# A short convolution and a spectral mix on one core: instruction order by hand, spectrum layouts and the band of the convolution changed

## The chip, the cores and the metric

The kernel runs on one core of one Trainium2 chip. The metric is the device time of one execution in microseconds; the time of a kernel is the median of its runs. A core has the engines TensorE (PE, whose weight loads are listed as PEld), VectorE (DVE), ScalarE (ACT), GpSimd (POOL) and SyncE (SP), each with its own queue that it issues in order. DMA transfers here are issued from POOL's queue (input x and the weights, with a cast from float32 to bfloat16) and from SP's queue (the filter and the output).

## The reference

Eight sequences of 3264 positions with 192 channels pass through two layers. The first is a causal convolution over 7 positions; each of 8 heads of 24 channels has one filter, normalised by a softmax. The second keeps the 64 lowest Fourier modes along the sequence, mixes the channels of each mode by a complex 192 x 192 matrix of its own, transforms back, and ends with a residual branch.

```python
# layer 1: x (8, 3264, 192), weight (8 heads, 7)
w = exp(weight - max(weight, -1)); w = w / (sum(w, -1) + 1e-09)
out = np.einsum('hk,bskhg->bshg', w, x_unf)     # x_unf: the 7 last positions
x = out.reshape(B, S, D)

# layer 2: w_r, w_i (64 modes, 192, 192), w_ch (192, 192)
X = np.fft.rfft(x, axis=1);  Xr, Xi = real and imaginary part of X[:, :64]
Yr = np.einsum('bmd,mde->bme', Xr, w_r) - np.einsum('bmd,mde->bme', Xi, w_i)
Yi = np.einsum('bmd,mde->bme', Xr, w_i) + np.einsum('bmd,mde->bme', Xi, w_r)
y = np.fft.irfft(Y, n=S, axis=1)                # Y is zero above mode 63
u = x + y
return u + np.maximum(u @ w_ch, 0.0)
```

## The kernel before

A batch is cut into 27 windows of 122 positions, each loaded with 6 positions of overlap ahead of it into 128 partitions of `x_all`. The unit of work is 10, 8 or 9 windows of a batch, 24 units in all, and each unit's load is one DMA issued on POOL (`load_unit`, L61).

*Setup.* `cband` (L123, L126) holds for each head a 128 x 128 band matrix with the filter's 7 values on its diagonals. It is built on DVE from seven masks (`maskk`, made on POOL at L105): one scaling and six multiply-adds for each head. `fst` is the DFT basis, 27 windows of 64 cosine and 64 sine columns: DVE computes the angle in five passes (L141 to L150, tiles `kprod` and `turns`), ACT takes Abs and two Sin (L152 to L154).

*Conv and DFT.* `conv_unit` takes a unit in two halves of four heads: four matmuls into a PSUM tile of a pool with two buffers (`cp`, L220), and an ACT copy back over `x_all` as bfloat16 (L226). For the first unit of a batch it first zeroes six rows of overlap on DVE (L215), once that unit has landed. `dft(b)` accumulates 27 matmuls of a batch (L272), casts the result to `xs` (L275), and `xtrans` turns it by six small matmuls into `xt`, the mixing's operand (L282 to L286). In program order dft(b) comes two batches behind the conv.

*Mixing and transposes.* 16 groups take four modes each: twelve matmuls (L321) of `xt` with the weights of two tiles `wt`, of which six buffers exist and 32 are loaded (L201); an ACT cast to `ymix`; two transposes, whose results go to `yeT` for two groups at once, one half by DVE (L343), one by ACT (L345), written with a stride. Between these stand `t_unit`, which transposes the conv's result into `cT` for the output (a tail copy `tl` on DVE, L233 to L236, 12 to 15 transposes on PE, L264, and two DVE copies, L266), and `g_part`, which transposes `fst` into the inverse basis `gst`.

*Output.* `zwi_pair` makes the mixed spectra of two batches, with and without `w_ch`, from `yeT` (L363 to L371). An item is two windows of two batches: `group_z` multiplies the inverse basis and `cT` into a PSUM tile (L379 to L386), ACT takes the maximum with zero in place (L388), `group_y` adds the rest (L393), DVE adds x into `t` (L404), and SP stores `t` after two items (L410). PSUM tiles here, those of `zwi_pair` (`zwps`) too, come from one pool of four buffers. group_y runs two items behind group_z in program order.

*The order.* Nothing above fixes the order on an engine. A planner orders the instructions of each engine by the program's order as a priority and by a model of when each is ready, so that instructions can pass each other; semaphores follow from the data.

## Time and profile before

| What | Value |
|---|---|
| median of 3 runs | 252.18 us |
| lowest, highest | 250.66, 253.94 us |
| the profiled execution: its own time | 252.29 us |
| its span, first to last instruction | 250.6 us |
| busy in the span: PE, DVE, ACT, POOL | 171.6, 131.7, 106.3, 69.7 us |
| mean granted PE clock | 0.890 of full speed |
| moved by DMA | 40.50 MB; 40.31 MB read from and 20.05 MB written to HBM |
| the chain that ended last, by engine | PE 50%, DMA 23%, DVE 7%, ACT 6%, POOL 5% |

All times in profile rows are microseconds from the span's start unless marked ns. A row of groups gives line, engine, operation, output and inputs, shapes and count, then busy time and mean of one in ns, then idle time of the engine just before them and what ended it. A row of a timeline gives start, length, engine, line and operation; the bracket at its end is the idle time before it and what ended that. L12 is line 12 of the kernel.

### The profile page before, as it was taken

The numbers are of one execution on the slowest core, as the hardware profiler recorded it, in microseconds if no ns is written. First come the engines' busy times: TensorE is split into PE (matmuls) and PEld (weight loads), VectorE is DVE, ScalarE is ACT, GpSimd is POOL, SyncE is SP. The second block draws the span as 40 slices with busy tenths as digits, with TensorE's granted clock in tenths as the row PEclk, the third lists the DMA queues.
The fourth block names the chain that finished last, engine by engine and source line by source line (L and its number), as shares of the span: only waits on it lengthen the run. The fifth ranks groups of instructions, "written<-read, shape, count | busy, mean of one in ns | idle before, by whom it ended". The sixth has DMA issues, their size and how long they took to land.

```text
span 250.6 us, 4371 instructions
## 1 busy us (share of the span) xinstructions
PE 171.6 (68%) x1699; PEld 130.4 (52%) x1699; DVE 131.7 (53%) x246; ACT 106.3 (42%) x140; POOL 69.7 (28%) x118
## 2 busy tenths in 40 slices
PE   0126604705999997797886359998798769978910
PEld 0014403604998995565653127886576447756700
DVE  4999022013334568589985121676656165756530
ACT  2025907502999935211221223655355345544510
POOL 8964445342900006756658100000000000000000
PEclk9999955665999999799999556999999999999995
DMA  4999999999980005999999900599898758799791
GB/s 37 171 188 191 192 192 192 192 192 188 132 137 1 3 3 67 179 191 158 160 166 157 157 0 0 150 258 263 218 253 230 208 158 237 214 257 255 203 260 56
DMA packets 65340, 40.50 MB, mean 162 GB/s; under 512 B 31016, under 2 KB 65320, under 8 KB 65320
## 3 DMA queue, kind: packets, MB, share of 16 engines
q0 software_dynamic: 37600, 20.14, 61.0%
q1 hardware_dynamic: 27720, 20.09, 29.0%
q8 instruction: 13, 0.21, 0.4%
q14 instruction: 7, 0.06, 0.1%
HBM read 40.31 MB, written 20.05 MB: 241 GB/s over the span
## 4 chain that ended last, share of the span: by engine, by line
PE 50%; DMA 23%; DVE 7%; ACT 6%; POOL 5%; issue 4%; SPq 1%; DVEq 0%; ACTq 0%; POOLq 0%
DMA x_all<-in_x_dram 19%; PE zp L379 7%; PE zp L386 7%; PE zp L384 7%; PE xp L272 7%; PE zp L393 6%; PE cp L220 5%; PE tp L264 5%; ACT zp L388 4%; DMA wt<-in_moe_w_i_dram 4%; DVE cT L266 4%; PE yp L321 2%; POOL x_all L61 2%; POOL wt L201 2%; SPq L410 1%
## 5 line engine op out<-in xcount | busy, mean ns | idle before, releaser
L404 DVE TENSOR_TENSOR t<-zp,x_all 122x768 f32<-122x768 f32 (+1 forms) x54 | 50.7, 955 | 33.2 <-PE zp L393 19.4
L388 ACT ACTIVATE zp<-zp 128x768 f32<-128x768 f32 x54 | 42.9, 795 | 40.9 <-PE zp L386 40.9
L226 ACT CAST x_all<-cp 122x960 bf16<-122x960 f32 (+2 forms) x48 | 39.4, 884 | 31.2 <-PE cp L220 30.9
L384 PE MATMUL zp<-win,cT 128*128 128x192 bf16 x216 | 45.8, 251 | 0.0
L220 PE MATMUL cp<-x_all,cband 128*128 128x240 bf16 (+2 forms) x192 | 30.2, 291 | 20.6 <-DVE cband L126 16.5
L379 PE MATMUL zp<-zwi,gst 128*128 128x384 bf16 x108 | 36.2, 335 | 3.7 <-ACT zwi L371 3.7
L220 PEld LDWEIGHTS <-cband 128*128 128x128 bf16 x192 | 19.8, 109 | 26.4 <-DVE cband L126 17.8
L393 PE MATMUL zp<-zwi,gst 128*128 128x384 bf16 x108 | 25.4, 324 | 8.8 <-ACT zp L388 8.8
L201 POOL DMA_DIRECT2D wt<-in_moe_w_r_dram x32 | 19.5, 610 | 42.4 <-PE yp L321 35.5
L266 DVE COPY cT<-tp 128x854 bf16<-128x854 bf16 (+2 forms) x48 | 28.3, 612 | 4.2 <-PE tp L264 3.7
L264 PE MATMUL tp<-ident,tl 122*128 122x122 bf16 x112 | 22.0, 227 | 10.1 <-DVE tl L233 9.8
L264 PE MATMUL tp<-ident,x_all 122*128 122x122 bf16 x216 | 26.3, 228 | 3.5 <-DVE cT L266 2.9
L61 POOL DMA_DIRECT2D x_all<-in_x_dram x24 | 23.6, 994 | 17.2 <-DMA x_all<-in_x_dram 17.1
L272 PE MATMUL xp<-x_all,fst 122*128 122x192 bf16 (+1 forms) x216 | 25.1, 263 | 0.8 <-ACT fst L154 0.8
L386 PEld LDWEIGHTS <-cT 128*128 128x128 bf16 x216 | 21.6, 100 | 7.6 <-issue 0.8
L384 PEld LDWEIGHTS <-cT 128*128 128x128 bf16 x216 | 21.6, 100 | 7.0 <-issue 4.7
L386 PE MATMUL zp<-win,cT 128*128 128x192 bf16 x112 | 23.6, 250 | 0.0
L386 PE MATMUL zp<-wB,cT 128*128 128x192 bf16 x104 | 22.2, 253 | 0.0
L264 PEld LDWEIGHTS <-x_all 122*128 122x128 bf16 x216 | 18.3, 103 | 7.4 <-issue 5.8
L272 PEld LDWEIGHTS <-fst 122*128 122x128 bf16 (+1 forms) x216 | 20.1, 105 | 2.1 <-ACT fst L154 1.2
L201 POOL DMA_DIRECT2D wt<-in_moe_w_i_dram x32 | 19.9, 621 | 2.2 <-DMA x_all<-in_x_dram 1.4
L326 ACT CAST ymix<-yp 128x192 bf16<-128x192 f32 x16 | 5.2, 327 | 34.5 <-PE yp L321 34.4
(82 smaller groups left out, 168.7 us busy)
## 6 DMA issues: line engine op xcount, KB each, us to landing
out_dram<-t SPq DMA_DIRECT2D x48, 336.0 KB
wt<-in_moe_w_r_dram POOLq DMA_DIRECT2D x32, 144.0 KB, 5.0
wt<-in_moe_w_i_dram POOLq DMA_DIRECT2D x32, 144.0 KB, 5.1
x_all<-in_x_dram POOLq DMA_DIRECT2D x8, 432.0 KB, 16.7
x_all<-in_x_dram POOLq DMA_DIRECT2D x9, 384.0 KB, 17.9
x_all<-in_x_dram POOLq DMA_DIRECT2D x7, 480.0 KB, 18.4
out_dram<-t SPq DMA_DIRECT2D x48, 30.0 KB
out_dram<-t SPq DMA_DIRECT2D x8, 168.0 KB
```

Of the source, the lines that this page charges most:

```text
L201: nc.gpsimd.dma_start(out=wt[64 * half:64 * half + 64, :, :, :], in_=src[MG * g:MG * g + MG, :, :].rearrange("m (p j) e -> p m j e", j=3))
L220: nc.tensor.matmul(cp[:, j, 0:GRP * n].rearrange("p (w e) -> p w e", w=n), cband[:, h, :], x_all[:, b, w0:w0 + n, GRP * h:GRP * h + GRP], ...
L226: nc.scalar.copy(out=dst, in_=srcv)
L264: nc.tensor.transpose(tp[:, WIN * k:WIN * k + WIN], slot_lhsT(b, u, tl, a + k), ident[0:WIN, 0:WIN])
L266: nc.vector.tensor_copy(out=cT[:, b, WIN * a:WIN * (a + cnt)], in_=tp[:, 0:WIN * cnt])
L272: nc.tensor.matmul(xp[:, 0:D], fst[0:k, c, :], x_all[0:k, b, c, :], start=(c == 0), stop=(c == NWIN - 1))
L379: nc.tensor.matmul(zp[:, k, 0:2 * D], gst[:, WIN * w:WIN * w + P], zwi[:, 2 * q:2 * q + 2, 0, :], start=True, stop=False, skip_group_check ...
L384: nc.tensor.matmul(o, cT[:, b, WIN * sa:WIN * sa + P], win0[:, 0:D], start=False, stop=False, skip_group_check=True)
L386: nc.tensor.matmul(o, cT[:, b, WIN * sb:WIN * sb + P], wBs[par], start=False, stop=(i == 1), skip_group_check=True)
L388: nc.scalar.activation(out=zp[:, :, 0:2 * D], in_=zp[:, :, 0:2 * D], func=ACT.Relu)
L393: nc.tensor.matmul(zp[:, k, 0:2 * D], gst[:, WIN * w:WIN * w + P], zwi[:, 2 * q:2 * q + 2, 1, :], start=False, stop=True, skip_group_check ...
L404: nc.vector.tensor_tensor(out=tv, in0=yv, in1=xv, op=ALU.add)
```

## The change

- Every engine issues in the order in which the program emits its instructions (`manual_schedule`); the program's order is rewritten for that.
- Setup: the two index rows are made first on POOL; the masks stand behind the loads of the first two units. `cband` is zeroed, and each diagonal of four heads is written at once by a copy under a mask; the filter's values stand in a PSUM tile (`wps`). The angle's passes follow on DVE without anything between; its three ACT functions (`make_f`) stand behind the evictions of the fourth conv unit.
- The DFT goes by units: `dft_unit` follows the conv with a lag of five units at first and one at the end; `xtrans` comes one unit after the batch's cast.
- Layouts: `fst` has cosine and sine of a mode side by side, and two selecting matrices `sel` take the place of `ident` and `perm` in `xtrans`. `xt` is laid out with the mode innermost, so that the copy into it is written in runs of 64 and the matmuls read its 32 columns 64 elements apart. `yeT` is laid out by mode and then part and batch; each group's two transposes go there by one DVE copy, and `zwi_pair` reads its columns 8 elements apart.
- Mixing: the weights of the third next group are asked for behind a group's matmuls. All transposes follow the spectrum, two units a group in the first eight groups and one in the next seven; `g_part` comes from the ninth group on.
- Output: the next `zwi_pair` follows the item of window 12 of a pair of batches in place of window 4.

```diff
+    ctx.enter_context(tc.manual_schedule())
...
-        for h in range(H):
-            nc.vector.tensor_scalar(out=cband[:, h, :], in0=maskk[:, 0, :], scalar1=wsb[:, h, 0:1],
-                                    scalar2=None, op0=ALU.mult)
-            for k in range(1, KK):
-                nc.vector.scalar_tensor_tensor(out=cband[:, h, :], in0=maskk[:, k, :],
-                                               scalar=wsb[:, h, k:k + 1], in1=cband[:, h, :],
-                                               op0=ALU.mult, op1=ALU.add)
+    nc.vector.memset(cband[:], 0.0)
...
+    wps = pxx.tile([P, 512], F32, tag="xp", name="wps")
+    wsb = wps[:, 0:H * KK].rearrange("p (h k) -> p h k", h=H)
...
+    for half in range(2):
+        hs = slice(4 * half, 4 * half + 4)
+        for k in range(KK):
+            nc.vector.copy_predicated(
+                out=cband[:, hs, :],
+                mask=maskk[:, k, :].bitcast(mybir.dt.uint16).unsqueeze(1).to_broadcast([P, 4, P]),
+                data=wsb[:, hs, k:k + 1].to_broadcast([P, 4, P]))
...
+    def make_f():
+        nc.scalar.activation(out=turns[:], in_=kprod[:], func=ACT.Abs)
+        nc.scalar.activation(out=fst[:, :, 1:2 * MODES:2], in_=kprod[:], func=ACT.Sin, scale=-TWOPI / S)
+        nc.scalar.activation(out=fst[:, :, 0:2 * MODES:2], in_=turns[:], func=ACT.Sin, scale=-TWOPI / S,
+                             bias=halfpi[:, 0:1])
...
-    xt = ep.tile([P, 3, MODES + 1, 2 * B], BF16, tag="xt")
+    xt = ep.tile([P, 4, 2 * B, MODES], BF16, tag="xt")
...
-    yeT = constp.tile([P, 2, B, 2 * MODES], BF16, tag="yeT")
+    yeT = constp.tile([P, 2, MODES, 2 * B], BF16, tag="yeT")
...
+    def dft_unit(b, u):
+        w0, n = UNITS[u]
+        if u == 0:
+            xps[b] = pxx.tile([P, 512], F32, tag="xp", name="xp")
+        xp = xps[b]
+        for c in range(w0, w0 + n):
             k = WIN if c < NWIN - 1 else LASTVALID
             nc.tensor.matmul(xp[:, 0:D], fst[0:k, c, :], x_all[0:k, b, c, :],
                              start=(c == 0), stop=(c == NWIN - 1))
+        if u == 2:
+            xs = workp.tile([P, D], BF16, tag="xs")
+            nc.vector.tensor_copy(out=xs[:], in_=xp[:, 0:D])
+            xps[b] = xs
...
+            for v in range(2):
+                nc.tensor.matmul(tp[64 * v:64 * v + 64, j, :], xsv[:, j, :], sel[:, v, :],
+                                 start=True, stop=True, tile_position=(0, 64 * v))
+        nc.vector.tensor_copy(out=xt[:, 0:3, b:2 * B:B, :],
+                              in_=tp[:, :, :].rearrange("p j (c m) -> p j c m", c=2))
...
+    for i, (b, u) in enumerate(units):
+        conv_unit(b, u)
+        if i == 3:
+            make_f()
+            setup_stack.close()
+        if xq:
+            xtrans(xq.pop(0))
+        dq.append((b, u))
+        lag = max(1, 5 - i // 4)
+        while len(dq) > lag:
+            db, du = dq.pop(0)
+            dft_unit(db, du)
+            if du == 2:
+                xq.append(db)
+    for db, du in dq:
+        dft_unit(db, du)
+        if du == 2:
+            xq.append(db)
+    for b in xq:
+        xtrans(b)
...
-                                 xt[:, j, m:m + 2, :].rearrange("p m k -> p (m k)"),
-                                 wt[:, m % MG, j, :], start=(j == 0), stop=(j == 2),
-                                 tile_position=(0, 32 * pos))
+                                 xt[:, j:j + 2, :, m].rearrange("p j k -> p (j k)"), wt[:, m % MG, j, :],
+                                 start=(j == 0), stop=(j == 2), tile_position=(0, 32 * pos))
+        for i in range(4 // MG):
+            n = 6 + (4 // MG) * g + i
+            if n < NGRP:
+                load_weights(n)
         ymix = workp.tile([P, D], BF16, tag="ymix")
         nc.scalar.copy(out=ymix[:], in_=yp[:, 0:D])
-        if tq:
-            t_unit(*tq.pop(0))
-        if gq:
+        for _ in range(2 if g < 8 else 1):
+            if tq and g < NG4 - 1:
+                t_unit(*tq.pop(0))
+        if gq and g >= 8:
             g_part(gq.pop(0))
...
+        nc.vector.tensor_copy(out=yeT[:, :, 4 * g:4 * g + 4, :],
+                              in_=et[:, :, :].rearrange("p t (q k) -> p t q k", q=4)[:, :, :, 0:16])
+        if g == NG4 - 2:
+            while tq:
+                t_unit(*tq.pop(0))
...
-        if item[2][0][1] == 4 and done_q + 1 < B // 2:
+        if item[2][0][1] == 12 and done_q + 1 < B // 2:
```

217 lines of the change are left out of this document (90 added, 127 removed).

## The prediction

> **What bounds the kernel now.** I read the busy times by stage first, because the share of the whole span hides that the stages have different limits. Columns: stage, its length, busy time (instructions) of PE, PEld, DVE, ACT and POOL, granted PE clock, DMA share, GB/s.
>
> ```profile
> 0.00:59.60 59.60, 19.18 (x114) 13.51 (x114) 26.77 (x91) 21.01 (x22) 32.95 (x55) 0.79 1.46 173
> 59.60:95.20 35.60, 34.44 (x387) 31.06 (x385) 17.31 (x17) 27.81 (x34) 6.42 (x11) 0.96 0.45 64
> 95.20:146.70 51.50, 37.52 (x537) 25.67 (x538) 34.86 (x81) 12.22 (x26) 30.37 (x52) 0.88 0.99 150
> 146.70:157.80 11.10, 9.72 (x56) 6.71 (x57) 2.97 (x4) 3.71 (x6) 0.00 (x0) 0.66 0.00 0
> 157.80:250.60 92.80, 70.75 (x611) 53.43 (x608) 49.82 (x54) 41.55 (x53) 0.00 (x0) 0.96 0.79 217
> ```
>
> Stage 1 loads x while PE is busy 19 of 60 us; stage 2 has PE busy 34 of 36 us and moves almost nothing; stage 3 streams the mixing weights; stage 4 starts the output, stage 5 stores it. So the work of stage 2 could lie beside the load of stage 1. The views of tile kprod (duration min/median/max in ns, first and last start) and of the waits (total, times, longest), and PE's timeline, say why it doesn't:
>
> ```profile
> L141 DVE TENSOR_TENSOR kprod<-sidx,midx x1: 1954/1954/1954, 20.5 to 20.5; 128x1728 f32<-128x1728 f32 x1
> L145 DVE TENSOR_SCALAR turns<-kprod x1: 1331/1331/1331, 22.5 to 22.5; 128x1728 f32<-128x1728 f32 x1
> L149 DVE TENSOR_TENSOR kprod<-kprod,turns x1: 1882/1882/1882, 31.1 to 31.1; 128x1728 f32<-128x1728 f32 x1
> L150 DVE TENSOR_SCALAR kprod<-kprod x1: 983/983/983, 38.0 to 38.0; 128x1728 f32<-128x1728 f32 x1
> L152 ACT ACTIVATE fst<-kprod x1: 1643/1643/1643, 39.1 to 39.1; 128x1728 bf16<-128x1728 f32 x1
> L153 ACT ACTIVATE turns<-kprod x1: 1626/1626/1626, 40.6 to 40.6; 128x1728 f32<-128x1728 f32 x1
> ```
>
> ```profile
> DVE x_all L215 <- DMA x_all<-in_x_dram: 28.7, 6, 6.4
> ```
>
> ```profile
> 44.76 4.21 PE L272 MATMUL xp<-x_all,fst 122*128 122x192 bf16 x27 [0.84 <-ACT fst L154]
> 48.81 0.68 PE L220 MATMUL cp<-x_all,cband 128*128 128x192 bf16 x6
> 59.15 0.32 PE L282 MATMUL tp<-ident,xs 128*64 128x128 bf16 x1 [9.66 <-DVE xs L275]
> ```
>
> DVE issues in order, and between the passes that build the DFT basis stand the small memsets of L215, each of which waits for a batch that has not landed: 28.7 us in six waits. The basis is therefore complete only at 44.7, and then PE waits another 9.7 us for a cast behind one more such memset. The load itself never pauses; its last piece lands at 63.1, where POOL's queue is released:
>
> ```profile
> 63.09 0.58 POOL L201 DMA_DIRECT2D wt<-in_moe_w_r_dram  x1 [1.49 <-DMA x_all<-in_x_dram]
> ```
>
> **Stage by stage, the change.** *The conv band.* Removed: 8 + 48 DVE passes over 128 numbers, which run from 5.6 to 20.6. Added: a memset and 14 predicated copies of 512 numbers, data in PSUM.
>
> ```profile
> L126 DVE SCALAR_TENSOR_TENSOR cband<-maskk,wsb,cband x48: 340/347/423, 6.1 to 20.3; 128x128 bf16<-128x128 bf16 x48
> L123 DVE TENSOR_SCALAR cband<-maskk,wsb x8: 251/419/679, 5.6 to 17.2; 128x128 bf16<-128x128 bf16 x8
> ```
>
> ```profile
> L404 DVE TENSOR_TENSOR t<-zp,x_all 122x768 f32<-122x768 f32 (+1 forms) x54 | 50.7, 955 | 33.2 <-PE zp L393 19.4 <-DMA out_dram<-t 12.1 <-ACT zp L388 1.4
> ```
>
> ```profile
> L321 PEld LDWEIGHTS <-xt x192: 92/96/151, 95.2 to 144.4; 128*32 128x32 bf16 x192
> L321 PE MATMUL yp<-wt,xt x192: 246/256/368, 95.2 to 144.5; 128*32 128x192 bf16 x192
> L286 DVE CAST xt<-tp x8: 1774/1796/1802, 59.7 to 93.4; 128x384 bf16<-128x384 f32 x8
> ```
>
> No row shows a predicated copy. The nearest is L404, two operands with one in PSUM: 955/768 = 1.24 ns a number, so 0.64 us each. The far end is L286, whose target is scattered: 1796/384 = 4.7 ns, 2.4 us each. A copy could hardly be quicker than L126's 347 ns. I take 0.64, since source and target run on in the free dimension; 14 cost 9.0 us. From about 6.0 (the masks now stand behind four loads on POOL, and each copy needs only its own mask) the band is done at 15.0, its first half at 10.5.
>
> *The basis.* L141 moves ahead, into the time in which DVE waits for the filter. The other passes follow the band with no memset between: 1.33 + 0.98 (the middle one counted like L150) + 1.88 + 0.98 = 5.2, to 20.2. On ACT the basis stands behind the evictions of four conv units, and the fourth unit's memset behind this chain on DVE; x is no hindrance, as 37 of 216 windows have landed by a sixth of 63.1. A microsecond for memset and first matmuls and 1.6 for its two evictions bring 22.8; table load, Abs and two Sin cost 1.28 + 1.63 + 1.64 + 1.64 = 6.2, so the basis is there at 29.0, not 44.7.
>
> ```profile
> 30.17 1.28 ACT L152 ACT_TABLE_LOAD   x1
> ```
>
> ```profile
> 65.00 4.80 ACT L226 CAST x_all<-cp 122x768 bf16<-122x768 f32 x6 [0.58 <-PE cp L220]
> 70.14 4.80 ACT L226 CAST x_all<-cp 122x768 bf16<-122x768 f32 x6 [0.34 <-PE cp L220]
> ```
>
> What is late next is ACT. In the old stage 2, conv and DFT together went at one batch (six evictions) in 70.14 - 65.00 = 5.14 us, 1.71 a unit, with PE full. Twenty units are left at 29.0: 34.3 us, to 63.3, which is just when the last x lands (63.1, plus the little that two iotas ahead of the first load take). Queued behind the basis on ACT are these evictions, and behind them conv and DFT on PE, so every microsecond that the band costs more moves this end by as much; that is the sensitive term. PE begins the DFT after a pause, and a batch of it took 4.21 us there (PE rows above), where conv and DFT of a batch together later took 5.14; I add 1.5 for that start. The last unit then needs its second eviction, nine DFT matmuls, cast, six transposing matmuls and the xt copy, now with runs of 64: about 3.5 us in all. The spectrum is complete at 63.3 + 1.5 + 3.5 = 68.3 instead of 95.2: a gain of 27.
>
> *Mixing and transposes.* All 24 units of transposes now come after the spectrum; before, some had been done early. A group mixes four modes, and the first eight groups carry two units each.
>
> ```profile
> 125.41 1.18 DVE L266 COPY cT<-tp 128x976 bf16<-128x976 bf16 x2
> 126.50 0.28 DVE L235 COPY tl<-x_all 122x512 bf16<-122x512 bf16 x1
> ```
>
> ```profile
> 129.88 0.60 PE tp L264 x8
> ```
>
> In the old order the tail copy of the next unit stood ahead of this unit's two copies (the tails of two buffers alternate). Written out by hand it stands behind them, and PE must wait for it with six of eight transposes: 0.28 + 0.49 + 1.09 = 1.85 us a unit, where DVE alone would need 1.4. With the one yeT copy (its 16-long runs cost me 0.3, not the 0.75 of before) a group takes 4.0, so the eighth ends at 68.3 + 32 = 100.3. Up to there the weights keep ahead; from there a group has one unit (2.4 us, basis transposes included) and the weights are late:
>
> ```profile
> 141.32 0.67 PE L321 MATMUL yp<-wt,xt 128*32 128x192 bf16 x10 [1.10 <-DMA wt<-in_moe_w_i_dram]
> ...
> 144.22 0.67 PE L321 MATMUL yp<-wt,xt 128*32 128x192 bf16 x10 [1.11 <-DMA wt<-in_moe_w_i_dram]
> ```
>
> ```profile
> 138.27 5.91 DMA wt<-in_moe_w_i_dram
> ...
> 146.67 0.48 PE zwps L363
> ```
>
> A group's weights arrive 2.90 us after the last one's. Those of the twelfth group can be asked for at 100.7, and land 6 us later, by the 5.91 from issue to landing; the last of 16 follow at 106.7 + 4 x 2.9 = 118.3, and 2.2 us more (2.45 now, less the shorter yeT copy) lead to the first zwps matmul at 120.5, against 146.7. So this stage takes 52 us as before: what the layouts save on DVE the serial tails take, and the weights come at their own pace.
>
> *Weight layout.* xt's 32 columns now lie 128 bytes apart instead of side by side. The nearest row is xs, read in steps of three elements:
>
> ```profile
> L282 PEld LDWEIGHTS <-xs x24: 120/122/178, 59.2 to 93.1; 128*64 128x64 bf16 x24
> ```
>
> 122 ns for 64 columns against 96 for 32: nothing that matters for 192 loads, so I count zero; the cover is PE's half microsecond of rest in each unit's cycle, and without it the rival below applies. The Trainium skill speaks against this layout (page "SBUF — State Buffer", section "Door 1: The DMA port swizzle"): a line is 16 bytes, and each access that goes on to another line pays a penalty, so that bf16 may be strided freely up to eight elements. It names no price, and no run here shows a step beyond that.
>
> *Output.* Stage 4 stays, without the four matmuls and the evictions of the second zwi pair (now at w = 12): 11.1 - 0.7 = 10.4. In stage 5 the rates tell what the order costs:
>
> ```profile
> 162.00:174.00 12.00, 12.00 (x109) 9.48 (x108) 8.19 (x9) 7.16 (x9) 0.00 (x0) 1.00 0.94 260
> 174.00:198.00 24.00, 19.83 (x170) 14.76 (x169) 13.56 (x15) 10.92 (x14) 0.00 (x0) 1.00 0.87 240
> 198.00:204.00 6.00, 2.85 (x21) 1.74 (x20) 3.21 (x4) 2.17 (x3) 0.00 (x0) 1.00 0.36 101
> ```
>
> ```profile
> 200.21 0.62 DVE L369 TENSOR_SCALAR zwi<-zwps,ascale 128x384 bf16<-128x384 f32 x1 [5.33 <-PE zwps L364]
> ```
>
> At 260 GB/s the stores are the bound; at 198 they starve, because the zwi scaling stands ahead of finished additions on DVE and waits 5.3 us for PE. A written order puts it behind them. All of stage 5 at 260 would be 92.8 x 217/260 = 77.5, but 6 us of the tail are draining. I take 86.5: the holes at 174 to 204 closed (24 x 20/260 + 6 x 159/260 = 5.5) and some 0.8 us of the rest. Range 84 to 93.
>
> **Sum.** 68.3 + 52.2 + 10.4 + 86.5 = 217.4 of span; the profiled execution lasts 252.29 for a span of 250.6, so 1.7 more: **219 us**. That execution lies 0.1 above the median 252.18, so no shift is made.
>
> **The rivals.**
> - *Stores keep their rhythm.* If the pauses come from four PSUM buffers, which a zwps tile shares wherever it stands, stages 4 and 5 stay 103.9, and the time is 226. For it: 240 GB/s in 174 to 198 too, away from the 5.3 us wait.
> - *Tails don't hold.* If DVE's 1.4 us a unit is reached, a group takes 3.1; the eighth ends 7 us sooner and the whole comes to 212. Against it: DVE is in order.
> - *Spread columns.* If each of xt's 32 columns costs what a scattered number costs in L286, 4.7 ns, a load takes 150 ns and twelve take 1.8 us a group; some 0.6 hides, and eight groups lose 1.2 each: 229. Later groups wait for weights anyway. It is the case that the Trainium skill's page "SBUF — State Buffer" leads one to expect.
> - *Copies scattered.* 14 x (2.4 - 0.64) = 24.6 more, unhidden: 244.
> - *Slower.* The same place, at a price beyond any row: slower by 2% starts at 257, that is 14 copies each 0.64 + 38/14 = 3.4 us, 6.6 ns a number. Broadcast data from PSUM, under a mask, is what could do it; the 4.7 of L286 speaks against. I put 260.
> - *The order doesn't change it.* If conv and DFT don't overlap the load on PE after all, stage 2 remains, and the time is about 250.
>
> **Numbers.** Forecast 0.53, its own range 212 to 226; stores 0.15; tails 0.12; spread columns 0.07; scattered copies 0.06; no change 0.03; slower 0.04. A change of under 2% is about what runs of 250.66 to 253.94 can't tell. Faster: 0.93, same 0.03, slower 0.04. The range 208 to 231 takes in the forecast, stores, tails and columns, with the ends of stage 5's range.
>
> **What will show it.** fst written before 30 us and DFT matmuls within the load; spectrum complete near 68; 24 transposed units at 1.85 us; first zwps near 120; no DVE wait of 5 us in the output, and 250 GB/s or more between its ends. A predicated copy well over 0.64 us, LDWEIGHTS of xt well over 0.1 us, or a first output later than 125 would make it wrong.

## The result and the profile after

The changed kernel takes 231.21 us (median of 4 runs, 230.27 to 232.54) where the kernel before takes 252.05 on the same chip: a ratio of 0.917, 95% interval 0.910 to 0.925. The forecast was 219 us with a range of 208 to 231; the time lies 12 us above the forecast and 0.2 above the range's end. The profiled execution lasts 230.81 us for a span of 229.1. Some executions take one to three per cent longer, most of them at a lower granted clock; the intervals leave them out, and where a median below carries its range, the range holds them.

The stages of the changed kernel by the busy times (stage, length, busy time and instructions of PE, PEld, DVE, ACT, POOL, granted PE clock, DMA share, GB/s), cut where the DFT begins, the spectrum is complete, the first zwps matmul starts, and the output begins to move:

```profile
0.00:31.70 31.70, 8.46 (x41) 5.26 (x42) 19.41 (x35) 15.57 (x15) 22.86 (x41) 1.00 1.34 157
31.70:75.90 44.20, 39.27 (x416) 34.01 (x416) 7.85 (x23) 32.34 (x40) 17.38 (x29) 1.00 1.36 172
75.90:131.80 55.90, 42.58 (x579) 32.54 (x579) 35.61 (x96) 8.19 (x20) 30.39 (x52) 0.85 0.94 139
131.80:141.50 9.70, 8.29 (x61) 6.52 (x62) 2.53 (x3) 3.96 (x6) 0.00 (x0) 0.82 0.00 1
141.50:229.10 87.60, 68.49 (x605) 53.42 (x603) 50.96 (x55) 41.30 (x53) 0.00 (x0) 0.94 0.84 230
```

The spectrum is complete at 75.9 instead of 95.2, a gain of 19.3; the mixing stage is 4.4 longer (55.9 for 51.5); the two output stages are 6.6 shorter (97.3 for 103.9). Together that is 21.5, the difference of the two spans. DVE's and ACT's timelines of the changed kernel show the setup (start, length):

```profile
5.68 10.40 DVE L163 CAST_PREDICATED cband<-maskk,wps 128x512 bf16<-128x512 uint16 x14
16.00 1.05 DVE L167 TENSOR_SCALAR turns<-kprod 128x1728 f32<-128x1728 f32 x1
...
20.42 1.06 DVE L172 TENSOR_SCALAR kprod<-kprod 128x1728 f32<-128x1728 f32 x1
```

```profile
24.50 1.66 ACT L176 ACTIVATE turns<-kprod 128x1728 f32<-128x1728 f32 x1
26.17 1.28 ACT L177 ACT_TABLE_LOAD   x1
27.46 2.11 ACT L177 ACTIVATE fst<-kprod 128x1728 bf16<-128x1728 f32 x1
29.45 2.18 ACT L178 ACTIVATE fst<-turns,halfpi 128x1728 bf16<-128x1728 f32 x1
```

Fourteen copies take 10.4 us; no memset stands between the angle passes any more, and the basis is ready at 31.6. What PE waits for in the changed kernel (total, times, longest):

```profile
PE xp L284 <- ACT fst L178: 6.2, 1, 6.2
PE tp L271 <- DVE tl L240: 5.4, 11, 0.7
...
PE yp L349 <- DMA wt<-in_moe_w_i_dram: 2.2, 3, 1.1
```

The 9.7 us behind the memset are gone. In their place PE waits 6.2 us for the basis itself, and in the mixing stage it waits for the tail copies. The tile views of xt and yeT hold the new layouts (ns min/median/max):

```profile
L349 PEld LDWEIGHTS <-xt x192: 130/174/233, 75.9 to 130.4; 128*32 128x32 bf16 x192
L298 DVE CAST xt<-tp x8: 557/558/559, 38.7 to 75.3; 128x384 bf16<-128x384 f32 x8
```

```profile
L366 DVE COPY yeT<-et x16: 212/216/227, 80.9 to 131.6; 128x128 bf16<-128x128 bf16 x16
```

The xt copy fell from 1796 to 558 ns; the weight loads rose from 96 to 174. In the store stage, finally, DVE's waits hold no zwps:

```profile
DVE t L425 <- PE zp L414: 15.7, 36, 1.1
DVE t L425 <- DMA out_dram<-t: 7.1, 8, 1.8
```

The longest wait is 1.8 us, where one of 5.3 stood before. The rate between the ends of the output stayed below the 250 GB/s that were put as a sign: 241 from 147 to 215 us, against 233 from 162 to 236 before. So direction and mechanism came as forecast, and two terms were too small: the spectrum came 7.6 us late (75.9 for 68.3), and the mixing stage took 3.7 more (55.9 for 52.2).

### The profile page after: what moved, and what is told of

Same layout as the page of the kernel before. It is cut to its first block, busy times and chain, and to the rows that moved or that the text cites. A ratio compares the mean times of both kernels' runs of the same rounds, so it can differ in the third digit from the quotient of the medians.

```text
span 229.1 us, 4342 instructions
## 1 busy us (share of the span) xinstructions
PE 167.1 (73%) x1699; PEld 131.8 (58%) x1699; DVE 116.4 (51%) x211; ACT 101.4 (44%) x132; POOL 70.6 (31%) x121
## 4 chain that ended last, share of the span: by engine, by line
DMA 33%; PE 31%; DVE 14%; POOL 8%; issue 3%; ACT 3%; SPq 3%; DVEq 0%; POOLq 0%; ACTq 0%
DMA x_all<-in_x_dram 16%; DMA out_dram<-t 8%; DVE cT L273 6%; PE tp L271 6%; DMA wt<-in_moe_w_i_dram 6%; DVE t L425 5%; PE zp L400 5%; PE zp L407 5%; PE zp L405 5%; POOL x_all L63 5%; PE zp L414 4%; DMA win<-in_moe_w_ch_dram 4%; SPq L431 3%; ACT x_all L233 2%; PE yp L349 2%
## 5 line engine op out<-in xcount | busy, mean ns | idle before, releaser
L425 DVE TENSOR_TENSOR t<-zp,x_all 122x768 f32<-122x768 f32 (+1 forms) x54 | 51.3, 957 | 32.3 <-PE zp L414 21.7
L409 ACT ACTIVATE zp<-zp 128x768 f32<-128x768 f32 x54 | 42.9, 795 | 31.4 <-PE zp L407 31.4
L405 PE MATMUL zp<-win,cT 128*128 128x192 bf16 x216 | 45.2, 249 | 0.0
L227 PE MATMUL cp<-x_all,cband 128*128 128x240 bf16 (+2 forms) x192 | 27.7, 286 | 19.7 <-DVE cband L163 15.2
L273 DVE COPY cT<-tp 128x854 bf16<-128x854 bf16 (+2 forms) x48 | 26.9, 590 | 18.3 <-PE tp L271 17.8
L63 POOL DMA_DIRECT2D x_all<-in_x_dram x24 | 23.8, 1001 | 15.9 <-DMA x_all<-in_x_dram 15.9
L271 PE MATMUL tp<-ident,tl 122*128 122x122 bf16 x112 | 23.2, 243 | 7.0 <-DVE tl L240 5.4
L211 POOL DMA_DIRECT2D wt<-in_moe_w_r_dram x32 | 19.3, 602 | 28.3 <-PE yp L349 21.7
L284 PE MATMUL xp<-x_all,fst 122*128 122x192 bf16 (+1 forms) x216 | 22.3, 252 | 7.4 <-ACT fst L178 6.2
L357 ACT CAST ymix<-yp 128x192 bf16<-128x192 f32 x16 | 5.1, 319 | 44.2 <-PE yp L349 44.2
L284 PEld LDWEIGHTS <-fst 122*128 122x128 bf16 (+1 forms) x216 | 18.4, 100 | 8.8 <-ACT fst L178 6.6
L407 PE MATMUL zp<-win,cT 128*128 128x192 bf16 x112 | 23.3, 248 | 0.0
L271 PEld LDWEIGHTS <-x_all 122*128 122x128 bf16 x216 | 18.9, 110 | 5.7 <-issue 4.8
L288 DVE CAST xs<-xp 128x192 bf16<-128x192 f32 x8 | 2.9, 358 | 34.3 <-PE xp L284 34.3
```

Of the source, the lines that this page charges most:

```text
L63: nc.gpsimd.dma_start(out=x_all[:, b, c0:c0 + n, :], in_=src)
L227: nc.tensor.matmul(cp[:, j, 0:GRP * n].rearrange("p (w e) -> p w e", w=n), cband[:, h, :], x_all[:, b, w0:w0 + n, GRP * h:GRP * h + GRP], ...
L271: nc.tensor.transpose(tp[:, WIN * k:WIN * k + WIN], slot_lhsT(b, u, tl, a + k), ident[0:WIN, 0:WIN])
L273: nc.vector.tensor_copy(out=cT[:, b, WIN * a:WIN * (a + cnt)], in_=tp[:, 0:WIN * cnt])
L284: nc.tensor.matmul(xp[:, 0:D], fst[0:k, c, :], x_all[0:k, b, c, :], start=(c == 0), stop=(c == NWIN - 1))
L405: nc.tensor.matmul(o, cT[:, b, WIN * sa:WIN * sa + P], win0[:, 0:D], start=False, stop=False, skip_group_check=True)
```

## The experiments

All are edits of the changed kernel. The first theory was that the spectrum's end follows the moment at which the basis is ready, and that the mixing stage is paced by the serial tails.

**1. The band built as before.** The 8 + 48 passes come back, in the new order.

```diff
-    for half in range(2): ... nc.vector.copy_predicated(out=cband[:, hs, :], ...)
+    for h in range(H):
+        nc.vector.tensor_scalar(out=cband[:, h, :], in0=maskk[:, 0, :], scalar1=wsb[:, h, 0:1], ...)
+        for k in range(1, KK):
+            nc.vector.scalar_tensor_tensor(out=cband[:, h, :], in0=maskk[:, k, :], ...)
```

> The changed kernel with the band built the old way: 8 scalings and 48 multiply-adds on DVE in place of a memset and 14 predicated copies. Theory A (backlog): in the changed kernel the basis is ready at 31.6 us, PE and ACT then owe 24 units of DFT and 19 of conv and run behind the load, which ends at 63.0; so what comes later on DVE ahead of the basis comes later at the end. The old band takes 15.0 us by the profile of before (5.6 to 20.6) against 10.4 + 0.5, 4 us more: spectrum (end of the last xt copy) at 80 in place of 75.9, total 4 us more, about 235. Rival B (the written order on PE, or the load, sets the end of the spectrum): spectrum stays within 1 us of 75.9, total about 231.

Measured: 239.24 us, ratio to before 0.953 (0.944 to 0.962). The passes took 21 us, from 5.7 to 26.8, not the 15 of before. DVE's timelines of this run and of the kernel before:

```profile
9.07 2.29 DVE L162 SCALAR_TENSOR_TENSOR cband<-maskk,wsb,cband 128x128 bf16<-128x128 bf16 x6
```

```profile
10.08 3.24 DVE L126 SCALAR_TENSOR_TENSOR cband<-maskk,wsb,cband 128x128 bf16<-128x128 bf16 x12
```

Here each pass writes what the one before it wrote, 2.29/6 = 380 ns apart; in the kernel before (second fence) the planner had run two heads by turns, 3.24/12 = 270 apart. So the run doesn't price the copies cleanly, but it moves the basis: 10.9 us later, and the spectrum 11.9 later.

**2. Three of the seven diagonals.** The other four copies of each half, and so most of the filter, are left out.

```diff
-        for k in range(KK):
+        for k in range(3):
```

> The changed kernel with 3 of the 7 diagonals of the band copied (6 predicated copies in place of 14; the other four positions of the filter are left out of the computation). Theory A: 8 x 0.743 = 5.9 us less on DVE ahead of the basis, spectrum at 70, total about 225. Rival B: spectrum stays at 75 to 76, total about 231.

Measured: 224.75 us (222.05 to 225.98), ratio 0.890 (0.880 to 0.901). The copies took 6.1 us less, the basis came 4.7 us earlier and the spectrum 3.7 earlier. Basis and spectrum's end move together in both directions, here by a little less than one to one.

**3. The basis ahead of everything.** The angle passes stand ahead of the band copies on DVE, Abs and Sin ahead of all evictions on ACT.

```diff
+    [the four passes on turns and kprod]
     for half in range(2): ... copy_predicated ...
-    [the four passes on turns and kprod]
...
+    make_f()
     units = [(b, u) for b in range(B) for u in range(3)]
```

> The changed kernel with one order altered: the angle's four passes stand ahead of the predicated copies on DVE, and the three ACT functions ahead of all evictions. Basis ready near 18 us, band ready near 21.5 instead of 16.1. Theory A: PE has its DFT work from the first unit on, 24 units of conv and DFT at about 1.75 us from 22 on end near 64 to 65, and the last load of 63.0 sets the rest: spectrum at 67 to 69, total 7 us less, about 224. Rival B: spectrum stays at 75 to 76 or becomes later by the 5 us by which the band is later, total 231 to 236.

Measured: 224.2 us (221.56 to 225.56), ratio 0.884 (0.874 to 0.895). The basis was there at 18.0, 13.6 earlier; the spectrum at 71.4, only 4.5 earlier. The theory in its first form falls: something else ends at 71.

**4. Each tail copy one unit ahead.**

```diff
-        tl = make_tail(b, u)
+        tl = tails.pop((b, u))
...
+            nxt = units.index((b, u)) + 1
+            if a == s0 and nxt < len(units):
+                tails[units[nxt]] = make_tail(*units[nxt])
             nc.vector.tensor_copy(out=cT[...
```

> The changed kernel with each unit's tail copy issued one unit ahead on DVE, before the two copies of the unit in front. Theory C (serial tails): a unit takes 1.4 us in place of 1.85, the eighth group of mixing ends 6 to 7 us sooner after the spectrum, the weights of the later groups are asked for sooner, and the first zwps matmul comes 4 to 6 us sooner than 131.8; total about 226. Rival D (the weights' stream sets this stage's length whatever DVE does): zwps within 1 us of 131.8, total about 231.

Measured: 222.61 us, ratio 0.884 (0.876 to 0.892). The mixing stage took 47.7 us instead of 55.9. PE's waits for tl are gone, and it waits for weights instead (PE's waits, then the windows of the stage):

```profile
PE yp L355 <- DMA wt<-in_moe_w_i_dram: 4.6, 7, 1.2
```

```profile
76.40:109.00 32.60, 28.07 (x441) 23.16 (x441) 27.20 (x76) 5.73 (x14) 24.75 (x43) 0.95 1.09 173
109.00:124.10 15.10, 10.29 (x140) 7.92 (x138) 7.63 (x22) 2.76 (x7) 5.75 (x10) 0.79 0.86 141
```

The 8.2 us are not all the edit's. The same code behind the spectrum took 52.7 to 53.9 us where the granted clock of the stage was 0.91 to 0.94 (runs 1, 2, 3, 9 and 13), and 54.8 to 55.9 where it was 0.84 to 0.87 (the changed kernel, runs 8, 10, 11, 14 and 17). Here it was 0.90; between run 1 (53.9 at 0.91) and run 8 (54.9 at 0.87) that leaves the edit some 6.4 us, an estimate, about what PE had waited for tl (5.4 and 1.6).

**5. The planner orders the new program.** Only the written order is taken out.

```diff
-    ctx.enter_context(tc.manual_schedule())
```

> The new program with the written order taken out: the planner orders the instructions again, as it did before; layouts, band copies and the order of the text stay. If the written order carries a good part of the gain (first theory), the basis stays early, since in the text no memset stands between its passes any more, but the planner is free to put memsets, evictions and the scaling of zwi ahead of finished work: I expect 238 us (233 to 246), with a wait for zwps of some 5 us back on DVE in the output, or a basis later than 35 us. If the layouts and the order of the text carry all of it (rival), the time stays at 229 to 233 and the basis at 31 to 33 us.

Measured: 240.36 us, ratio 0.951 (0.948 to 0.955). DVE's timeline shows what the planner does with the band copies:

```profile
12.94 1.48 DVE L162 CAST_PREDICATED cband<-maskk,wps 128x512 bf16<-128x512 uint16 x2
18.98 0.14 DVE L221 MEMSET x_all<- 6x96 uint32 x1 [4.56 <-DMA x_all<-in_x_dram]
19.05 4.37 DVE L162 CAST_PREDICATED cband<-maskk,wps 128x512 bf16<-128x512 uint16 x6
25.85 0.14 DVE L221 MEMSET x_all<- 6x96 uint32 x1 [2.44 <-DMA x_all<-in_x_dram]
```

A memset that waits for x stands among the copies, as it once stood among the angle passes. The basis was ready at 20.2, but the band only at 29.4, and the DFT began at 32.1. The spectrum comes at 87.5, and the output takes 101.7 us instead of 97.3 (94.9 to 98.9 in all runs with the written order and the same output), with 7.2 us of waits for zwps on DVE, the longest 3.9. The mixing stage is shorter (50.8), since some transposes again run before the spectrum. So of the 21 us of the whole change some 9 are the written order's.

**6. The units spread evenly over the groups.**

```diff
-        for _ in range(2 if g < 8 else 1):
-            if tq and g < NG4 - 1:
+        for _ in range(2 - g % 2):
+            if tq:
...
-        if g == NG4 - 2:
-            while tq:
-                t_unit(*tq.pop(0))
```

> One edit in the mixing stage: the 24 units of transposes are spread as 2, 1, 2, 1 ... over the 16 groups instead of 2 in each of the first eight and 1 in each of the rest. Theory (each unit costs its serial 1.85 us wherever it stands, and the later groups wait for weights that were asked for late): 24 x 1.85 + 16 x 0.3 = 49 us plus about 1 for the transposes of the basis, so the stage from first yp to first zwps takes 50 us instead of 55.9 and the whole 226 us (224 to 228). Rival (the weights' own rate sets the end of the stage): the stage stays at 54 to 56 us and the whole at 230 to 232.

Measured: 224.79 us, ratio 0.888 (0.884 to 0.892); the mixing stage took 51.0 us, near the 50 of the theory. Its granted clock was 0.93, though, and at that clock run 2 took 53.0 without the edit, so the edit is worth some 2 us of the 4.9. The rate of the weights was not the bound, as the same bytes came in less time; run 12, below, shows that better.

**7. xt side by side.**

```diff
-    xt = ep.tile([P, 4, 2 * B, MODES], BF16, tag="xt")
+    xt = ep.tile([P, 3, MODES + 1, 2 * B], BF16, tag="xt")
...
-                xt[:, j:j + 2, :, m].rearrange("p j k -> p (j k)")
+                xt[:, j, m:m + 2, :].rearrange("p m k -> p (m k)")
```

> xt alone goes back to the layout of before: the 32 columns of a weight load side by side, and a scattered copy. The copy takes 1.80 us instead of 0.56, which counts once, behind the last unit: spectrum 1.2 us later. The 192 weight loads go from 174 back to about 96 ns. Theory (the loads are mostly hidden: twelve matmuls of a group took 0.53 against 0.43 us): at most 16 x 0.1 = 1.6 us come back, so 230 to 232.5 in all. Rival (the loads lie on the path in full): 192 x 78 ns = 15 us come back, and the time is 216 to 220.

Measured: 234.1 us, ratio 0.927 (0.923 to 0.930). The tile view of xt and the windows up to the spectrum and through the mixing stage:

```profile
L349 PEld LDWEIGHTS <-xt x192: 92/97/151, 80.4 to 134.5; 128*32 128x32 bf16 x192
L298 DVE CAST xt<-tp x8: 1761/1789/1803, 39.7 to 78.6; 128x384 bf16<-128x384 f32 x8
```

```profile
31.70:80.40 48.70, 40.32 (x416) 34.78 (x416) 17.55 (x23) 32.36 (x40) 17.82 (x29) 0.95 1.26 158
80.40:135.90 55.50, 43.37 (x580) 31.80 (x580) 36.21 (x97) 8.20 (x20) 30.34 (x52) 0.78 0.94 140
```

Loads back at 97 ns leave the mixing stage at 55.5, at a granted clock of 0.78; run 15, with the spread columns and a clock of 0.79, took 55.8. So the 78 ns a load are hidden, and the rival falls. The new copy is worth more than its 1.2 us at the end: with the old one the spectrum comes 4.5 us later, because on DVE the memset for the next batch's first conv stands behind each copy, and PE waits for it (3.3 us in this stage, 1.1 in the changed kernel). About a microsecond of the 4.5 is left over; the granted clock, 0.50 from 31 to 36 us, may be half of it: runs 4 and 11, with 0.53 and 0.50 there and the copy of the changed kernel, had the spectrum at 76.4 and 76.5.

**8. As 3, with the DFT one unit behind the conv.**

```diff
-        lag = max(1, 5 - i // 4)
+        lag = 1
```

> The edit of the third run (angle passes ahead of the band copies, basis ahead of all evictions on ACT), and besides the DFT follows the conv by one unit from the start instead of five and then fewer. Theory (what sets the spectrum's end is the moment at which the DFT's 24 units begin, at 1.69 us a unit, where in the third run they began at 28.5 us because of the distance of five): DFT from about 23 us, spectrum at 23 + 24 x 1.69 + 2.4 = 66 us (65 to 68.5) instead of 71.4, the whole 219 us (217 to 222). Rival (evictions on ACT or x's landing keep the pace, so that an earlier start of the DFT only opens pauses in it): spectrum at 70 to 72 us, the whole at 223 to 225.

Measured: 224.22 us, ratio 0.888 (0.882 to 0.893). The DFT began at 23.8, and still the spectrum came at 70.8; the rival was right. POOL's tile view of maskk and its timeline, in this run, give one cause:

```profile
L109 POOL TENSOR_SCALAR_AFFINE_SELECT maskk<-ones_b x7: 286/1104/2037, 4.9 to 9.8; 128x128 bf16<-128x128 bf16 x7
```

```profile
10.92 3.84 POOL L63 DMA_DIRECT2D x_all<-in_x_dram  x4
...
65.88 0.58 POOL L210 DMA_DIRECT2D wt<-in_moe_w_r_dram  x1 [1.51 <-DMA x_all<-in_x_dram]
```

The same views of the changed kernel:

```profile
L109 POOL TENSOR_SCALAR_AFFINE_SELECT maskk<-ones_b x7: 282/282/298, 4.9 to 6.4; 128x128 bf16<-128x128 bf16 x7
```

```profile
6.66 3.85 POOL L63 DMA_DIRECT2D x_all<-in_x_dram  x4
...
63.04 0.58 POOL L211 DMA_DIRECT2D wt<-in_moe_w_r_dram  x1 [1.45 <-DMA x_all<-in_x_dram]
```

The mask selects now run beside the angle passes and take up to 2 us each instead of 0.28, 6.0 in all instead of 1.8; the four loads behind them are asked for at 10.9 instead of 6.7, and the last x lands at 65.9 instead of 63.0. The Trainium skill (page "SBUF — State Buffer", section "Who interferes with whom") says that DVE and GpSimd share a pair of ports as a lock: a DVE instruction that runs in a two-port mode, or that reads two inputs from SBUF beside a GpSimd instruction that reads SBUF, contends with it, and the later of the two waits until the other is done. The trace agrees: the selects lie beside the four passes, from 4.9 to 11.0 us, and the longest, 2037 ns, is about as long as the subtraction of two SBUF tiles, 1.96 us. Late in the stage the load costs PE one wait, behind the last batch's memset:

```profile
PE cp L226 <- DVE x_all L221: 1.3, 1, 1.3
```

**9. The passes between the two halves of the band.** As 8, but behind the selects in time.

```diff
     for half in range(2):
         for k in range(KK): ... copy_predicated ...
+        if half == 0:
+            [the four passes on turns and kprod]
```

> As the eighth run, but the four angle passes stand between the two halves of the band copies on DVE, behind the seven mask selects of POOL instead of beside them. In the third and eighth runs these selects took 6.04 us instead of 1.77, the loads queued behind them on POOL were asked for 4.25 us later, and the last x landed at 65.9 instead of 63.0. Theory (the passes hold POOL up, the load then sets the spectrum's end, at 4.9 us behind its last landing): selects back to 1.8 us, last x near 63.0, spectrum near 68 us instead of 70.75, the whole 221 to 222 us. Rival (the spectrum's end in the eighth run is the pace of PE and ACT, not the load): the load ends at 63 again, but the spectrum at 70 to 71, and the whole at 223 to 225.

Measured: 223.36 us (221.14 to 226.72). The selects took 1.76 us in all and the last x landed at 62.6, so the cause of the late load is shown. But the spectrum came at 71.6: PE's wait of 1.3 us is gone, and the DFT began 2.2 us later than in run 8. So the load is not the bound here, and the rival was right again. PE's windows say what is:

```profile
26.00:32.00 6.00, 5.71 (x50) 5.05 (x48) 0.36 (x1) 4.41 (x7) 1.98 (x3) 1.00 1.60 192
32.00:45.00 13.00, 12.42 (x138) 10.83 (x138) 2.67 (x8) 11.20 (x14) 5.12 (x6) 1.00 1.60 192
45.00:63.00 18.00, 17.13 (x187) 15.02 (x185) 3.03 (x9) 15.69 (x20) 6.24 (x14) 1.00 1.57 193
```

From the DFT's first matmul to 63 us PE is busy 95% of the time. A basis that comes before the conv has begun saves nothing more, because all of the conv is then still owed.

**10. The copies by turns.**

```diff
-    for half in range(2):
-        for k in range(KK):
+    for k in range(KK):
+        for half in range(2):
```

> The 14 predicated copies alternate between the two halves of the band instead of doing one half after the other, so that no copy writes what the one before it wrote. Theory (the 743 ns from one copy to the next hold 50 to 60 ns in which a copy waits for the one before, as the band passes of before took 270 ns each in turns of two heads, and 380 one head after the other in the first run): 14 copies in 14 x 0.64 = 9.0 to 9.7 us, the angle passes 0.7 to 1.4 us earlier. Rival (a copy takes 743 ns whatever it writes): 10.4 us, and all else as in the changed kernel.

Measured: 226.36 us (one execution). DVE's timeline:

```profile
5.66 8.46 DVE L163 CAST_PREDICATED cband<-maskk,wps 128x512 bf16<-128x512 uint16 x14
```

8.5 us for the fourteen, 604 ns apart instead of 743: the theory, and more than it expected. (Each pair of copies also reads the same mask now; the run doesn't tell that apart from what they write.) Basis and spectrum came 1.7 us earlier.

**11. The second zwi pair at w = 4 again.**

```diff
-        if item[2][0][1] == 12 and done_q + 1 < B // 2:
+        if item[2][0][1] == 4 and done_q + 1 < B // 2:
```

> The second zwi pair at w = 4 again, as before, in the written order. Theory (the written order alone keeps its scaling off finished additions): the output takes 97 to 98 us from first zwps to the end, as in the changed kernel, and the whole 230 to 232. Rival (its place closed the holes): a wait of about 5 us for zwps comes back on DVE, the output takes 100 to 103 and the whole 234 to 237.

Measured: 231.73 us, ratio 0.917 (0.911 to 0.923), against 231.21. DVE waits for zwps once, at the very start of the output:

```profile
DVE zwi L390 <- PE zwps L385: 1.7, 1, 1.7
```

The place is worth nothing that these times can tell; the written order keeps the scaling off finished additions. Its output took 99.5 us by the trace, 0.6 beyond the other runs' longest, at a granted clock of 0.56 in the first 8.5 of them.

**12. All that helped so far:** the edits of 9, 4 and 6 together.

> All that helped at once: the ninth run's order of band, passes, basis and DFT, each tail copy one unit ahead, and the units spread 2, 1, 2, 1 over the groups. If the three gains add up: spectrum 68, mixing stage 45 (43 to 48, since DVE alone would need 24 x 1.4 + 16 x 0.5 = 42 and the weights moved at up to 203 GB/s), output 96 to 98, and 1.7 around the span: 211 us (208 to 214). If the weights' landing binds as soon as the units go faster, the mixing stage stays at 48 to 50 and the whole comes to 215 to 217.

Measured: 217.7 us, ratio 0.862 (0.858 to 0.866): spectrum 71.2, mixing stage 46.0, output 98.3. The mixing stage came as expected; the spectrum stood at 71 as in 3, 8 and 9.

```profile
71.20:117.20 46.00, 36.62 (x580) 29.57 (x580) 34.59 (x96) 8.19 (x20) 30.37 (x52) 0.96 1.08 177
```

Against run 9, which lacks the two mixing edits (53.0 us at a granted clock of 0.94), they are worth 7.0 us together.

What ends there was open, and five runs more went to it. **13. Conv ahead while the basis is made**, with DVE evicting in ACT's place:

```diff
-            nc.scalar.copy(out=dst, in_=srcv)
+            i = 3 * b + u
+            if i < 3 or (i >= 7 and half == 0):
+                nc.scalar.copy(out=dst, in_=srcv)
+            else:
+                nc.vector.tensor_copy(out=dst, in_=srcv)
...
-        if i == 3:
+        if i == 2:
             make_f()
...
-        lag = max(1, 5 - i // 4)
+        lag = max(1, 6 - max(0, i - 6) // 3)
```

> The changed kernel with another hand for the conv's evictions: ACT does the first three units and then the basis, DVE the next four, and from the eighth unit on each does one half; the DFT follows at a distance of six units, later fewer. Band copies and angle passes stay. The basis comes at about 28.9 us instead of 31.6 (two evictions fewer ahead of it), but 7 conv units are then done instead of 5. Theory (the spectrum ends when PE has done what it still owes once the basis is there): 17 conv units and 24 DFT units at 0.9 us or little less, 36 us, to 65, and 2.4 us for the rest; the load, which ends at 63, allows 68. Spectrum at 68 (67 to 70), the whole 223 to 224. Rival (only the moment counts at which the DFT begins, 1.69 us a unit): 28.9 + 24 x 1.69 + 2.4 = 72, the whole 227 to 228.

**14. Run 9 with every second eviction on DVE:**

```diff
-            nc.scalar.copy(out=dst, in_=srcv)
+            if half == 0:
+                nc.scalar.copy(out=dst, in_=srcv)
+            else:
+                nc.vector.tensor_copy(out=dst, in_=srcv)
```

> The ninth run with every second eviction of the conv on DVE instead of ACT. Theory (PE's own work binds: it was busy 35.3 of 37.0 us from 26 to 63): the spectrum comes at most 1 to 1.5 us earlier, by the stalls of 0.21 and 0.37 us on evictions that end, at 70 to 71, and the whole stays at 222 to 223.5. Rival (ACT's 48 evictions of 0.88 us, 42 us behind the basis at 23.7, bind): the spectrum falls to the load's end and what follows it, 68, the whole 219 to 220.5.

**15. Run 13 with the copies of run 10:**

> e13 with the band copies by turns between the halves. If PE's debt binds in e13, the 1.9 us that the copies save (tenth run) move the basis to 27 us and the spectrum by 1 to 2 us, until the load's end allows no less than 67.9; the whole 222 to 223. If the load binds in e13 already, nothing changes against it.

**16. Run 15 with the tails of 4 and the spread of 6:**

> e15 with each tail copy one unit ahead and the units spread 2, 1, 2, 1 over the groups, as in the twelfth run. Spectrum as in e15 (68), mixing stage as in the twelfth run (46.0), output 97 to 98, and 1.7: 213 us (211 to 215). If the spectrum stays at 71: 216 to 218, no better than the twelfth run.

Measured: 13, 223.95 us (221.71 to 228.49; ratio 0.881, 0.876 to 0.885), spectrum 72.4; 14, 227.95 us (223.71 to 230.06), spectrum 74.2; 15, 225.56 us (ratio 0.895, 0.890 to 0.899), spectrum 70.7; 16, 215.83 us (213.95 to 218.49; ratio 0.853, 0.848 to 0.858), spectrum 71.6, mixing stage 45.8. So runs 12 and 16 beat both kernels; whether 16 beats 12 is within their spread. The expected 68 was reached by none. In run 14 ACT was busy 19.7 of 48.5 us and the spectrum came later, not earlier (in its one trace, of the execution of 230.06 us, at a granted clock of 1.00 up to there): half the evictions on DVE stand in line with the memsets that PE waits for.

```profile
PE cp L227 <- DVE x_all L222: 3.5, 6, 0.6
```

So ACT's 48 evictions by themselves are not the bound, and in run 13 the same line cost 3.1 us of what conv gained by running ahead. The windows from the first DFT matmul to the complete spectrum can be set side by side:

| run | DFT begins | spectrum | PE matmuls between | us | us a matmul |
|---|---|---|---|---|---|
| changed kernel | 31.7 | 75.9 | 416 | 44.2 | 0.106 |
| 1 | 42.5 | 87.8 | 416 | 45.3 | 0.109 |
| 2 | 27.0 | 72.2 | 416 | 45.2 | 0.109 |
| 3 | 28.5 | 71.4 | 419 | 42.9 | 0.102 |
| 4 | 31.7 | 76.4 | 416 | 44.7 | 0.107 |
| 6 | 32.5 | 77.8 | 416 | 45.3 | 0.109 |
| 8 (late load) | 23.8 | 70.8 | 442 | 47.0 | 0.106 |
| 9 | 26.0 | 71.6 | 442 | 45.6 | 0.103 |
| 10 | 30.0 | 74.2 | 416 | 44.2 | 0.106 |
| 11 | 31.3 | 76.5 | 416 | 45.2 | 0.109 |
| 12 | 25.9 | 71.2 | 444 | 45.3 | 0.102 |
| 13 | 30.6 | 72.4 | 405 | 41.8 | 0.103 |
| 14 | 25.7 | 74.2 | 442 | 48.5 | 0.110 |
| 15 | 28.4 | 70.7 | 406 | 42.3 | 0.104 |
| 16 | 29.0 | 71.6 | 405 | 42.6 | 0.105 |

With the DFT beginning anywhere from 24 to 43 us, the time behind it is 0.102 to 0.110 us for each matmul that PE then still owes. (Run 5, whose order is the planner's, and run 7, with the scattered copy, lie outside, at 0.114 and 0.117.) The counts differ by a tenth only, so the table alone can't tell a debt of matmuls from some 45 us that are always needed. Runs 9 and 12 begin 3 to 5 us before 13 and 16 and end at the same time, because they owe 37 to 39 matmuls more. (By this price run 13's own 41 units and 405 matmuls come to 42 us, where I had put 36 + 2.4: the run did what it was built for, and its expectation was too low.) The next run tests the debt itself.

**17. A sixth of the owed matmuls left out.**

```diff
         for c in range(w0, w0 + n):
+            if c % 3 == 1:
+                continue
```

> The changed kernel with every third matmul of the DFT left out (9 of 27 windows of each batch, so that the spectrum lacks them); conv, evictions, casts and everything behind stay as they are. 72 of the 416 matmuls that PE owes at 31.7 us are gone. Theory (PE's owed work sets the end, at 0.106 us a matmul): 344 x 0.106 = 36.5 us, spectrum at 68.2 instead of 75.9, just above the 68 that the load allows, and the whole 223.5 us. Rival (the chain from conv to eviction to DFT sets the pace, and PE only looks busy): spectrum at 73 to 76, the whole 228 to 231.

Measured: 226.17 us (224.5 and 227.83), spectrum at 72.8: 3.1 us earlier, where the theory said 7.7 and the rival nothing to 2.9. Its granted clock was 0.54 from 31 to 36 us, where the changed kernel had 1.00; against runs 4 and 11, with that dip and all matmuls, the window is 3.5 to 4 us shorter. And 0.106 is too high a price for these: in run 9 ten DFT matmuls start at 60.56 and the next ones at 61.40, 0.084 each, so that 72 are 6.0 us. PE's waits from 31 to 71 us:

```profile
PE cp L227 <- ACT x_all L233: 2.9, 10, 0.5
PE xp L286 <- ACT x_all L233: 1.0, 1, 1.0
```

PE now waits for evictions more than twice as often. So the table is a description of one balance: PE's owed work comes first, but the hand-over from conv to eviction through two PSUM buffers lies only 3 to 4 us behind it. The load's end with what follows it (62.6 to 63, and the 4.9 us by which run 8's spectrum came behind its last landing) would allow 68, an estimate, another 4 to 5 us earlier. What more buffers for cp, or the memsets off DVE's queue, would bring was not tried.

## Why the prediction was right and wrong

*Right: direction, order of the causes, output.* The basis no longer stands behind memsets; conv and DFT lie beside the load (last x at 63.0, as put); the stores keep closer to their rate: zwps to the end took 97.3 us for 96.9. That it came so near is in part luck: with the same output code the runs took 94.9 to 98.9, and the rate of 250 GB/s was not reached. Run 5 shows that the written order does this, and run 11 that the second pair's place doesn't. The rival by which the stores keep their rhythm, 103.9 us, is out.

*Off: the copy, 0.64 us.* One copy is 0.69 us long and the next starts 743 ns after it, so fourteen took 10.4 instead of 9.0. I priced a lone instruction; the row of the old band passes, 347 ns long and yet some 270 apart, could have told that the spacing depends on the neighbours. Run 10 shows it: 604 ns by turns. The rivals of scattered copies fall.

*Off: the basis, 29.0.* It was ready at 31.6: the copies' 1.4 us later, and Sin at 2.11 and 2.18 us instead of 1.64 and 1.74, now that it writes every second column of fst (no run takes that alone); the rest is the evictions ahead of it.

*The step that failed: "Twenty units are left at 29.0: 34.3 us".* With the start and the last unit's 1.5 and 3.5 us that made 39.3; it took 44.2. A unit of that price is one conv and one DFT: 17 matmuls, and with the six of each batch's xtrans twenty units make 388. But the conv of five units had been done ahead, and no DFT at all, so 19 conv units and all 24 DFT units were owed: 416 matmuls, 28 more. At the mean of 0.106 us that is 3.0 of the 4.9 us; as 36 DFT matmuls more, at 0.084, and eight of the conv less, it is nearer 2.2, both estimates. The other 1.9 to 2.7 is the pace, 0.106 instead of 0.101 a matmul; what made it slower stays open. With the 2.7 by which the DFT began later (31.7 for 29.0) that makes the 7.6. I took the queue on ACT for the sensitive term; runs 9 and 14 speak for PE's debt, and run 17 confirms it for some 3 to 4 us, with ACT's hand-over close behind.

*Half right: the mixing stage.* Its two parts in the changed kernel, the groups with two units and those with one:

```profile
75.90:108.40 32.50, 24.57 (x332) 18.94 (x332) 22.22 (x59) 2.54 (x8) 18.68 (x32) 0.85 0.93 136
108.40:131.80 23.40, 18.01 (x249) 13.60 (x247) 13.39 (x38) 5.65 (x12) 11.72 (x20) 0.85 0.95 142
```

The first eight groups took 32.5 us for the 32 put, and run 4 shows the tails as the cause, so that the rival by which the tails don't hold is out. The nearness is in part luck: in run 9, at a granted clock of 1.00, the same eight took 30.2 (71.6 to 101.8), so at that clock 1.85 us a unit is somewhat high. The later eight took 23.4 instead of 20.2 up to the first zwps, and 22.8 in run 9, where the clock from 103 us on was 0.84; this is the second term that was too small. That they are held by weights asked for late may be right in kind (runs 4 and 6 ask sooner, and in run 12, with both edits, the stage is 7.0 us shorter than in run 9), but the 2.9 us a group, taken from the old order, was too little: the yp of the ninth group began at 108.4 and that of the last at 130.3 with its weights, 3.1 us a group, though PE waited for weights only three times, 2.2 us in all. Which part is weights and which DVE is not told apart.

*Right for the sum, off in price: the spread columns.* I counted nothing for weight loads that went from 96 to 174 ns. The Trainium skill's 16-byte line (page "SBUF — State Buffer", section "Door 1: The DMA port swizzle") agrees in direction with the trace, 78 ns for 32 columns at a step of 128 bytes. Runs 7 and 15, 55.5 and 55.8 us at clocks of 0.78 and 0.79, show that next to none of it reaches the path here.

*The range.* Its upper end came from one missed term at a time. Two were missed at once, both in the same direction, and the sum passed it by a hair. Three of the signs that it named came out against it: a first zwps at 131.8, past the 125; weight loads of xt at 174 ns; a basis at 31.6 instead of before 30.

## What to carry to other kernels

When a pipeline is started late, count what each stage still owes at that moment in instructions, not in units that hold both stages; the debt of the later stage is the whole of it. An input brought forward pays only until the next queue is reached: here the third, eighth and ninth run moved the basis by 8 to 14 us for 4 to 5 us of spectrum, and two mixing changes that cost nothing (a tail copy one unit ahead, units spread evenly) paid 7 together. Before two stages of two traces are compared, compare the granted clock in them: here the same code took 52.7 us at 0.94 and 55.9 at 0.85. Price a chain of instructions by the spacing of its neighbours, and look for small waiting instructions in front of large ones on an engine that issues in order.

## What the runs showed of the hardware

- Predicated copies of 512 numbers with their data in PSUM last 0.69 us; they start 743 ns apart when each writes what the last one wrote, 604 when they write two halves by turns (run 10). The same holds for the band passes: 380 (run 1) and 270 ns (the kernel before).
- Angle passes in float32 on DVE slowed POOL's selects from 0.28 us to 2.04 at most, and so delayed loads that stood behind them by 4.25 us (runs 3 and 8; gone in run 9).
- Sin over 128 x 1728 took 2.11 to 2.18 us where it writes every second bf16 column, and 1.64 to 1.74 where it writes runs of 64.
- A weight load of 32 columns 128 bytes apart takes 174 ns instead of 96; it is hidden here beside matmuls of 256 and more (runs 7 and 15).
